# A first MLP product with high and low input halves side by side, and a gate moved from the weights to the output rows

## The chip, the cores and the metric

The kernel runs on one core of a Trainium2 chip. The metric is the device time of one execution in microseconds (us). A profile of one execution gives the span (first to last instruction) and every instruction's start and length on five engines: PE (TensorE, matrix products), DVE (VectorE), ACT (ScalarE), POOL (GpSimd) and SP (which issues most of the transfers). PEld stands for weight loads on TensorE.

## The reference, cut to what matters

```python
x = A_x                                             # 2048 x 512, float32
sa, ca, ga, sb, cb, gb = split(silu(c) @ w_mod, 6)  # six rows of 512
h = layernorm(x) * (1 + ca) + sa
x = x + ga * irfft2(rfft2(h) * (w_r + 1j * w_i))    # spectral filter
h = layernorm(x) * (1 + cb) + sb
act = mish(h @ w1 + b1)                             # w1: 512 x 1376; mish(u) = u * tanh(softplus(u))
x = x + gb * (act @ w2)                             # w2: 1376 x 512
```

The change is in the last two lines: the MLP and its gate `gb`.

## The kernel before, in words

The spectral part comes first: a forward transform, a product with the filter, and the back transform, whose last step (`p3_col`, `p3_row`) adds into x, which stays in SBUF as 16 row groups of 128 rows. While that last step runs (16 steps, from about 111 to 166 us), the kernel also prepares the MLP: `load_w1` and `split_w1`, `load_w2`, `gate_w2`, `split_w2` and `sum_w2` are spread over its steps by the table `prep`. Everything is in an order written out by hand: each engine runs its instructions in the order in which the code records them, and waits for semaphores where it needs another engine's result.

To multiply with nearly float32 accuracy at the rate of the format that TensorE reads faster (`F32R`), each operand is split into a high part (the value cast to that format) and a low part (the rest). Of the four products, high x high, low x high and high x low are kept.

The MLP works on 8 blocks of 256 rows. A block's hidden features (1376 = 10 x 128 + 96) are taken in 6 groups, t0 to t5, of which t0 has the tile of 96 and the others two tiles of 128. So there are 48 steps, and step s is done by `mlp(s)`. In it:

- `up(s)` (L720) is the first product: for each tile, 12 matmuls of 256 columns (three kinds of product, four parts of the 512 input features). Both tiles of a group fill the two halves of one PSUM bank with tag A, of which there are two.
- `mish(s)` (L730) reads that bank: ACT applies the activation with the bias to each tile (L736). For t1 to t5, DVE then makes four sums and differences of 128-wide pieces (L749): rows of a block and groups of features are combined so that `down` needs 7 products in place of 8. ACT casts the 7 pieces to their high parts (L755, two instructions), and `low` (L759, L761) takes the low parts on DVE.
- `down(s - 2)` is the second product for the group two steps back (L784; L770 for t0), which adds up over the block in six PSUM banks.
- In t1 the previous block is finished: `gather` (L787) copies four partial sums to `p` and `q` in SBUF on ACT, `residual` (L799, L802) adds the two others to x on DVE, and `spread` (L814) does the remaining additions into x on POOL: two between partial sums (L796, L797) and four into rows of x (L808 to L811). `store` sends both row groups out.
- In t3, `norm_pair` normalises the next block's two row groups on ACT (L141). In t4 and t5, `transpose_in` (L610) transposes half of them each, into an A bank and ahead of `up`, and `split_in` (L620) applies scale and shift on ACT (L625), takes the high part on DVE (L629) and the low part on DVE (L630).

The gate `gb` is a row of 512 factors, `gbr`, the same on every partition. It is multiplied into the rows of w2 as they are loaded: `gate_w2` (L677, L680) on POOL, 13 instructions of up to 128 x 512. What `down` makes is then already gated.

Small buffers come from a pool with two of each tag: `y` holds loaded rows of w2, `h` normalised rows and `p`, `q`, `g1` the activations, `g2` the sums. Whoever takes a third waits until the first is free. The end (`finish`, L847) does the last block's sums on DVE around the last `down`, whose products are taken without the 7-for-8 scheme (L777), with L691 giving the low parts of its weights.

## Time and profile before

| | us |
|---|---|
| median of 3 runs | 416.37 (414.9 to 416.45) |
| the profiled execution | 415.98 |
| its span | 414.2 |
| busy: PE, DVE, ACT, POOL | 394.8, 281.2, 220.8, 152.0 |
| mean granted TensorE clock | 0.989 |
| all transfers | 35.25 MB, a mean of 85 GB/s |

How to read what follows. The chain of work that ended last is followed back from the last instruction, at each step to what released it, and is shown in order of time: start, length, engine, output, line, number of instructions. A row of a timeline has start, length, engine, line, operation, output <- inputs, shapes and number of instructions; in brackets is the idle time of the engine ahead of it and what ended that. A row of a group of instructions ends with the busy time, the mean length of one in nanoseconds, and the idle time before them. A row of the page's slices has one digit for each fortieth of the span, the busy share in tenths. Rows with two times and a colon are stretches of time with the busy time of PE, PEld, DVE, ACT and POOL, the granted TensorE clock, and the transfers.

### The profile page before, as it was taken

The page shows a single profiled execution, that of the slowest core. Times are in us where ns is not written, and L with a number is a line of the kernel's source. Part 1 is how long each engine was busy: PE and PEld are TensorE (multiplying, and loading weights), DVE is VectorE, ACT ScalarE, POOL GpSimd, SP SyncE. Part 2 cuts the span into 40 slices and gives each one's busy share as a digit, 9 for nine tenths or more (in the row PEclk, how much of TensorE's full clock was granted, in tenths as well). Part 3 has the DMA queues.
Part 4 walks back from the last instruction along what each step waited for, and adds up shares of the span by engine and source line. Part 5 has one row for each costly group of instructions (what it writes and reads, how often), then busy time and mean ns, then how long its engine had stood idle before and what let it go on. Part 6 is the DMA issues. An engine that isn't in the chain of part 4 may idle for free.

```text
span 414.2 us, 8147 instructions
## 1 busy us (share of the span) xinstructions
PE 394.8 (95%) x3152; PEld 381.5 (92%) x3152; DVE 281.2 (68%) x542; ACT 220.8 (53%) x499; POOL 152.0 (37%) x180
## 2 busy tenths in 40 slices
PE   8999889999999899999999889999999999999996
PEld 8888778899899899899999789999999999999995
DVE  1999949686259999896854644673673772862854
ACT  1677754576746655655643653463472563553441
POOL 0677725576246975560500500410400500500520
PEclk9999999999999999999999969999999999999999
DMA  8999871371303322010100100010000000000021
GB/s 272 354 354 377 244 255 52 101 294 66 101 21 117 94 96 68 5 53 2 51 2 2 51 0 2 2 51 2 22 31 0 27 27 0 28 27 0 32 73 51
DMA packets 20902, 35.25 MB, mean 85 GB/s; under 512 B 3712, under 2 KB 6560, under 8 KB 20480
## 3 DMA queue, kind: packets, MB, share of 16 engines
q1 hardware_dynamic: 20432, 34.21, 24.3%
q8 instruction: 25, 0.41, 0.4%
q10 hardware_dynamic: 432, 0.53, 0.4%
q14 instruction: 13, 0.11, 0.1%
HBM read 30.53 MB, written 4.19 MB: 84 GB/s over the span
## 4 chain that ended last, share of the span: by engine, by line
PE 65%; DVE 23%; ACT 6%; issue 2%; DMA 2%; POOL 1%; SPq 0%; DVEq 0%; POOLq 0%; ACTq 0%
PE bank L727 26%; PE bank L784 21%; DVE st L112 4%; PE bank L456 3%; PE bank L502 3%; DVE ve L125 3%; DVE buf L749 2%; PE bank L770 2%; DVE x L651 2%; PE bank L489 2%; DMA x<-in_A_x_dram 2%; PE bank L435 1%; DVE w2a L691 1%; DVE buf L227 1%; DVE buf L207 1%
## 5 line engine op out<-in xcount | busy, mean ns | idle before, releaser
L761 DVE TENSOR_TENSOR al<-buf,ah 128x512 fp32r<-128x512 f32 (+2 forms) x87 | 64.6, 763 | 34.7 <-ACT ah L755 31.4
L755 ACT CAST ah<-buf 128x512 fp32r<-128x512 f32 (+2 forms) x87 | 46.1, 552 | 77.2 <-PE bank L784 34.8
L749 DVE TENSOR_TENSOR buf<-buf 128x128 f32<-128x128 f32 x156 | 56.8, 405 | 44.4 <-ACT buf L736 43.0
L796 POOL TENSOR_TENSOR buf<-buf 128x256 f32<-128x256 f32 x7 | 5.2, 738 | 163.4 <-ACT buf L791 163.4
L736 ACT ACTIVATE buf<-bank,b1n 128x256 f32<-128x256 f32 (+1 forms) x88 | 37.1, 468 | 41.8 <-PE bank L727 41.8
L727 PE MATMUL bank<-h,w1h 128*128 128x256 f32 (+1 forms) x352 | 55.0, 290 | 1.8 <-ACT buf L736 1.8
L727 PE MATMUL bank<-h2o,w1h 128*128 128x256 f32 (+1 forms) x352 | 53.5, 283 | 0.8 <-DVE h2o L629 0.8
L727 PEld LDWEIGHTS bank<-h,w1h 128*128 128x128 f32 (+1 forms) x352 | 47.9, 193 | 2.6 <-ACT buf L736 2.2
L727 PEld LDWEIGHTS bank<-h2o,w1h 128*128 128x128 f32 (+1 forms) x352 | 46.4, 186 | 1.3 <-DVE h2o L629 1.0
L784 PE MATMUL bank<-w2a,ah 128*128 128x256 f32 x168 | 36.3, 283 | 0.0
L784 PE MATMUL bank<-w2b,ah 128*128 128x256 f32 x161 | 34.4, 283 | 0.0
L727 PE MATMUL bank<-h,w1l 128*128 128x256 f32 (+1 forms) x176 | 28.8, 288 | 0.0
L784 PEld LDWEIGHTS bank<-w2a,ah 128*128 128x128 f32 x168 | 28.2, 191 | 0.0
L727 PE MATMUL bank<-h2o,w1l 128*128 128x256 f32 (+1 forms) x176 | 28.0, 282 | 0.0
L784 PEld LDWEIGHTS bank<-w2b,ah 128*128 128x128 f32 x161 | 26.8, 192 | 0.0
L680 POOL TENSOR_TENSOR buf<-buf,modr 128x512 f32<-128x512 f32 (+1 forms) x13 | 17.9, 1386 | 21.4 <-DMA buf<-in_B_w_dram 21.2
L234 PE MATMUL bank<-buf,mring 128*128 128x512 f32 x48 | 21.4, 445 | 4.2 <-DVE buf L227 1.9
L112 DVE BATCH_NORM_STATS2 st<-x 128x6 f32<-128x512 f32 x32 | 22.0, 688 | 5.0 <-DMA x<-in_A_x_dram 4.6
L638 PE MATMUL bank<-kc,d 128*128 128x128 f32 x128 | 24.8, 276 | 0.5 <-ACT d L360 0.5
L639 PE MATMUL bank<-kc,d 128*128 128x128 f32 x128 | 24.7, 275 | 0.0
L727 PEld LDWEIGHTS bank<-h,w1l 128*128 128x128 f32 (+1 forms) x176 | 24.6, 193 | 0.0
L727 PEld LDWEIGHTS bank<-h2o,w1l 128*128 128x128 f32 (+1 forms) x176 | 23.8, 186 | 0.0
(203 smaller groups left out, 1001.4 us busy)
## 6 DMA issues: line engine op xcount, KB each, us to landing
buf<-in_B_w_dram SPq DMA_DIRECT2D x20, 256.0 KB, 2.7
xring<-in_x_t_dram SPq DMA_DIRECT2D x16, 256.0 KB, 4.7
x<-in_A_x_dram SPq DMA_DIRECT2D x16, 256.0 KB, 5.0
wm<-in_w_mod_dram SPq DMA_DIRECT2D x16, 256.0 KB, 4.4
out_dram<-x SPq DMA_DIRECT2D x16, 256.0 KB, 2.0
mraw<-in_km_dram SPq DMA_DIRECT2D x16, 128.0 KB, 4.8
wqa<-in_w_q_dram SPq DMA_DIRECT2D x8, 256.0 KB, 4.2
wqb<-in_w_q_dram SPq DMA_DIRECT2D x8, 256.0 KB, 5.2
```

The source lines that it names most:

```text
L112: nc.vector.bn_stats(t, x[:, n, :])
L125: nc.vector.scalar_tensor_tensor(out, a, one, r, op0=op, op1=ALU.mult)
L234: nc.tensor.matmul(pa, m[:, a, 0:128], g, start=(i == 0), stop=False)
L638: nc.tensor.matmul(o, dj[:, 0:128], kc[0][:, n, :], start=True, stop=False)
L639: nc.tensor.matmul(o, dj[:, 64:192], kc[1][:, n, :], start=False, stop=True)
L680: nc.gpsimd.tensor_tensor(r, r, gbr[:r.shape[0]], op=ALU.mult)
L727: nc.tensor.matmul(ps[:rows, 256 * e:256 * e + 256], w[:, k, f * P:f * P + rows], h[:, k, :], start=(i == 0), stop=(i == 11))
L736: nc.scalar.activation(w[:rows, c], ps[:rows, c], AF.Mish, bias=b1n[:rows, f:f + 1])
L749: nc.vector.tensor_tensor(o, p, q, op=op)
L755: nc.scalar.copy(h, r)
L761: nc.vector.tensor_tensor(l, r, h, op=ALU.subtract)
L784: nc.tensor.matmul(o, a[p][:, e], w2[t][q][:, r], start=(half is None and t == 1 and i == 0), stop=(last and i == 2 and (n, half) != (1, 0)))
```

## The change

The first product takes its input with the high and low parts of each of the four feature parts side by side, as 512 columns. One matmul with the high weights makes high x high in the left half of a bank and high x low in the right half; a matmul of 256 columns with the low weights adds low x high to the left half. A tile takes 8 matmuls in place of 12 and fills a whole A bank. ACT then copies the right half with the bias to SBUF, DVE adds the left half, and one Mish on ACT works on both tiles in SBUF.

The gate no longer goes into w2: `gate_w2` is gone, and the rows that come out of the second product are multiplied by `gbr`. For that the output rows are put together apart from x: `own_rows` on DVE after `gather`, then in `chain` on POOL the other sums and two products with the gate, then `add_rows` adds to x on POOL. In the last block all of it is on DVE, and the last products are gated from PSUM.

The high part of the next block's input is taken on ACT in place of DVE. `transpose_in` stands behind `up` in place of ahead of it, and `split_in` between Mish and the casts. The steps of w2's preparation are moved: t1 by one step earlier, t2 and t3 by one or two, and the last split of t3 from after the loop to step 14.

```diff
     def h2_tiles(b):
         if b % 2 == 0:
-            h2[b] = [pm.tile([P, 4, 256], F32R, name=f"h2{i}", tag=f"h2{i}") for i in range(2)]
+            h2[b] = pm.tile([P, 4, 2, 256], F32R, name="h2e")
...
     def split_in(n, g):
-        hh, hl = (v[:, 2 * g:2 * g + 2, :] for v in h2[n // 2])
-        nc.vector.tensor_copy(hh, tv)
+        hh, hl = (h2[n // 2][:, 2 * g:2 * g + 2, i, :] for i in range(2))
+        nc.scalar.copy(hh, tv)
         nc.vector.tensor_tensor(hl, tv, plain(hh), op=ALU.subtract)
...
-    def gate_w2(t, *es):
-        for e in es:
-            r = st["w2", t][e]
-            nc.gpsimd.tensor_tensor(r, r, gbr[:r.shape[0]], op=ALU.mult)
...
     def up(g):
         b, t = divmod(g, NT)
-        ups[g] = ps = bank("C" if g < 2 else "A")
-        hh, hl = h2[b]
-        parts = [(w, h, k) for w, h in ((w1h, hh), (w1l, hh), (w1h, hl)) for k in range(4)]
+        h = h2[b]
+        ups[g] = []
         for e, f, rows in tiles(t):
-            for i, (w, h, k) in enumerate(parts):
-                nc.tensor.matmul(ps[:rows, 256 * e:256 * e + 256], w[:, k, f * P:f * P + rows], h[:, k, :],
-                                 start=(i == 0), stop=(i == 11))
+            ps = bank("C" if g < 2 and e == 0 else "A")[:rows]
+            fs = slice(f * P, f * P + rows)
+            for k in range(4):
+                nc.tensor.matmul(ps, w1h[:, k, fs], h[:, k], start=(k == 0), stop=False)
+            for k in range(4):
+                nc.tensor.matmul(ps[:, 0:256], w1l[:, k, fs], h[:, k, 0], start=False, stop=(k == 3))
+            ups[g].append((e, f, ps))

     def mish(g):
...
-        for e, f, rows in reversed(tiles(t)):
-            c = slice(256 * e, 256 * e + 256)
-            nc.scalar.activation(w[:rows, c], ps[:rows, c], AF.Mish, bias=b1n[:rows, f:f + 1])
+        for e, f, ps in ups.pop(g):
+            rows = ps.shape[0]
+            o = w[:rows, 256 * e:256 * e + 256]
+            nc.scalar.activation(o, ps[:, 256:], AF.Identity, bias=b1n[:rows, f:f + 1])
+            nc.vector.tensor_tensor(o, o, ps[:, 0:256], op=ALU.add)
+        o = w[:rows, 0:256 * e + 256]
+        nc.scalar.activation(o, o, AF.Mish)
...
-    def chain(b, eng):
-        p, q = done[b]
+    def own_rows(b):
+        r = buf("y"), buf("y")
+        nc.vector.tensor_tensor(r[1], out_ps[b][1], done[b][0], op=ALU.add)
+        nc.vector.tensor_copy(r[0], out_ps[b][2])
+        return r
+
+    def chain(b, eng, r):
+        p, q = done.pop(b)
         eng.tensor_tensor(q[:, 0:256], q[:, 0:256], p[:, 0:256], op=ALU.add)
         eng.tensor_tensor(q[:, 256:], q[:, 256:], q[:, 0:256], op=ALU.add)
...
+        both = q[:, 256:].unsqueeze(1).to_broadcast([P, 2, 256])
+        v = r[0].rearrange("p (j d) -> p j d", j=2)
+        if b == NB - 1:
+            eng.tensor_copy(v, both)
+        else:
+            eng.tensor_tensor(v, v, both, op=ALU.add)
+        eng.tensor_tensor(r[0][:, 256:], r[0][:, 256:], p[:, 256:], op=ALU.add)
...
+            eng.tensor_tensor(r[1][:, 256:], r[1][:, 256:], q[:, 0:256], op=ALU.add)
+            for t in r[::-1]:
+                eng.tensor_tensor(t, t, gbr, op=ALU.mult)
+
+    def add_rows(b, eng, r, rows=(1, 0)):
+        for i in rows:
+            n = 2 * b + i
+            eng.tensor_tensor(x[:, n, :], x[:, n, :], r[i], op=ALU.add)
...
     def mlp(s):
         b, t = divmod(s, NT)
         nxt = 2 * b + 2 if b < NB - 1 else None
+        up(s)
         if t in (4, 5) and nxt:
             transpose_in(nxt, t - 4)
-        up(s)
-        if t in (4, 5) and nxt:
-            split_in(nxt, t - 4)
         if t == 3 and nxt:
             norm_pair(nxt)
         parts = mish(s)
+        if t in (4, 5) and nxt:
+            split_in(nxt, t - 4)
+        parts = high(s, parts)
         down(s - LAG)
         if t == 1 and b:
             gather(b - 1)
-            residual(b - 1)
+            r = own_rows(b - 1)
         low(parts)
         if t == 1 and b:
-            spread(b - 1)
+            chain(b - 1, nc.gpsimd, r)
+            add_rows(b - 1, nc.gpsimd, r)
             store(b - 1)
...
     def finish():
...
-        own, ahead, far, both = rows_of(b)
-        chain(b, nc.vector)
-        far(nc.vector)
-        own(nc.vector)
-        both(nc.vector)
+        r = buf("y"), buf("y")
+        chain(b, nc.vector, r)
+        add_rows(b, nc.vector, r)
         down(total - 1)
-        residual(b, (0,))
-        store(b, (0,))
-        ahead(nc.vector)
-        residual(b, (1,))
-        store(b, (1,))
+        for i in range(2):
+            nc.vector.tensor_tensor(r[i], out_ps[b][2 - i], gbr, op=ALU.mult)
+            add_rows(b, nc.vector, r, (i,))
+            store(b, (i,))
...
-    for t, s in ((1, 1), (2, 6), (3, 11)):
-        for lag, fn, *args in ((-1, load_w2, t), (0, gate_w2, t, 0), (1, gate_w2, t, 1), (2, split_w2, t, False),
-                               (2, sum_w2, t, 0, 1), (3, sum_w2, t, 2, 3), (5, split_w2, t, True)):
-            if s + lag < N2:
-                prep[s + lag].append((fn, args))
...
+    for t, *at in ((1, 0, 2, 2, 3, 5), (2, 4, 8, 6, 7, 9), (3, 9, 11, 11, 12, 14)):
+        for s, fn, *args in zip(at, (load_w2, split_w2, sum_w2, sum_w2, split_w2), (t,) * 5,
+                                (None, False, 0, 2, True), (None, None, 1, 3, None)):
+            prep[s].append((fn, [a for a in args if a is not None]))
```

The new function `high` holds the casts that stood at the end of `mish`.

More of the change, by code (lines that the diff above doesn't have):

```diff
@@ L601, in h2_tiles @@
         if b % 2 == 0:
[L602 removed]
+            h2[b] = pm.tile([P, 4, 2, 256], F32R, name="h2e")
         else:
[L604 to L605 removed]
+            h2[b] = big.tile([P, 4, 2, 256], F32R, name="h2o", tag="cr")
     def norm_pair(n):
@@ L750, in mish, with high @@
             parts = [(w[:, P:], slice(0, 3)), (u, slice(3, 7))]
+        return parts
+    def high(g, parts):
+        hi, lo = acts[g] = [act.tile([P, 7, P], F32R, name=n) for n in ("ah", "al")]
         flat = []
@@ L792, in gather @@
         done[b] = p, q
-    def chain(b, eng):
-        p, q = done[b]
+    def own_rows(b):
[5 more added lines that the diff above has]
+        p, q = done.pop(b)
         eng.tensor_tensor(q[:, 0:256], q[:, 0:256], p[:, 0:256], op=ALU.add)
         eng.tensor_tensor(q[:, 256:], q[:, 256:], q[:, 0:256], op=ALU.add)
-    def residual(b, rows=(1, 0)):
-        for r in rows:
-            n = 2 * b + r
-            nc.vector.tensor_tensor(x[:, n, :], x[:, n, :], out_ps[b][2 - r], op=ALU.add)
@@ L900, in tile_spectral_block @@
             split_in(0, s - 7)
-    low(mish(0))
+    low(high(0, mish(0)))
     split_w2(0, False)
-    low(mish(1))
-    split_w2(3, True)
+    low(high(1, mish(1)))
     load_w2(4)
-    gate_w2(4, 0, 1)
     sum_w2(4, 0, 1, 2, 3)
@@ L922, in tile_spectral_block @@
             load_w2(5)
-            gate_w2(5, 0, 1)
         if s == total - 3:
```

36 lines of the change are left out of this document (10 added, 26 removed).

## The prediction, made before the changed kernel had run

> **What bounds the kernel now.** I read the page first, then the chain of work that ended last, then the timelines of one block of the MLP on each engine.
>
> ```profile
> PE 394.8 (95%) x3152; PEld 381.5 (92%) x3152; DVE 281.2 (68%) x542; ACT 220.8 (53%) x499; POOL 152.0 (37%) x180
> ...
> PE   8999889999999899999999889999999999999996
> ...
> PE 65%; DVE 23%; ACT 6%; issue 2%; DMA 2%; POOL 1%; SPq 0%; DVEq 0%; POOLq 0%; ACTq 0%
> ```
>
> The chain in order of time (start, length, engine, line, instructions):
>
> ```profile
> 296.08 1.38 PE bank L770 x6
> ...
> 323.70 2.84 PE bank L727 x24
> 326.54 1.38 PE bank L770 x6
> ...
> 330.76 2.52 PE bank L784 x21
> ...
> 407.45 2.76 PE bank L777 x12
> ```
>
> From about 186 us to the end the chain is almost only TensorE: `up` (L727) and `down` (L770, L784) back to back. A block of 256 rows takes 326.54 - 296.08 = 30.46 us. One 256-wide matmul takes 2.84/24 = 118 ns, a 512-wide one 1.38/6 = 230 ns, weight load included: the loads are hidden behind the streams.
>
> So the other engines matter only where TensorE waits for them. Their timelines around the first groups of the block's MLP (t1 to t3; t1 is the group in which the previous block is gathered):
>
> ```profile
> 321.02 0.28 PE L784 MATMUL bank<-w2c,ah 128*128 128x256 f32 x1
> 321.22 0.84 ACT L736 ACTIVATE buf<-bank,b1n 128x256 f32<-128x256 f32 x2 [2.50 <-PE bank L727]
> 322.09 1.02 DVE L749 TENSOR_TENSOR buf<-buf 128x128 f32<-128x128 f32 x4 [2.92 <-ACT buf L736]
> 323.66 1.04 ACT L755 CAST ah<-buf 128x384 fp32r<-128x384 f32 x2 [1.60 <-issue]
> 323.74 1.28 DVE L802 TENSOR_TENSOR x<-x,bank 128x512 f32<-128x512 f32 x2 [0.63 <-PE bank L784]
> 324.60 1.19 ACT L791 COPY buf<-bank 128x256 f32<-128x256 f32 x4
> 324.94 1.71 DVE L761 TENSOR_TENSOR al<-buf,ah 128x384 fp32r<-128x384 f32 x2
> 325.37 0.73 POOL L796 TENSOR_TENSOR buf<-buf 128x256 f32<-128x256 f32 x1 [24.25 <-ACT buf L791]
> 327.22 1.29 POOL L808 TENSOR_TENSOR x<-x,buf 128x512 f32<-128x512 f32 x1
> 328.58 0.75 POOL L809 TENSOR_TENSOR x<-x,buf 128x256 f32<-128x256 f32 x1
> 329.28 0.80 POOL L810 TENSOR_TENSOR x<-x,buf 128x256 f32<-128x256 f32 x1
> 330.16 1.43 POOL L811 TENSOR_TENSOR x<-x,buf 128x512 f32<-128x512 f32 x1
> 327.45 2.98 DVE L749 TENSOR_TENSOR buf<-buf 128x128 f32<-128x128 f32 x4 [0.80 <-ACT buf L736]
> 330.35 2.25 DVE L761 TENSOR_TENSOR al<-buf,ah 128x384 fp32r<-128x384 f32 x2
> 330.46 0.62 ACT L755 CAST ah<-buf 128x512 fp32r<-128x512 f32 x1 [2.16 <-DVE buf L749]
> 330.99 1.52 ACT L141 ACTIVATE buf<-x,nmr,rstd 128x512 f32<-128x512 f32 x2
> 339.59 1.21 DVE L761 TENSOR_TENSOR al<-buf,ah 128x384 fp32r<-128x384 f32 x2 [1.10 <-ACT ah L755]
> ```
>
> The reader is to see two things. First, while POOL works (325.37 to 331.59) the four 128-wide DVE operations of L749 take 2.98 us in place of 1.02, and the two of L761 take 2.25 in place of 1.21: a DVE operation with two SBUF inputs gets through about once per POOL instruction. Second, none of this reaches TensorE: the next `up` finds a free bank, since a group fills one A bank of two.
>
> An operation that reads PSUM is not held up in this way: 0.68 us, inside a POOL instruction of 2.25.
>
> ```profile
> 150.51 2.25 POOL L596 TENSOR_TENSOR w1l<-buf,w1h 128x512 fp32r<-128x512 f32 x1
> 151.56 0.68 DVE L651 TENSOR_TENSOR x<-x,bank 128x512 f32<-128x512 f32 x1
> ```
>
> The SBUF — State Buffer page of the Trainium skill (Who interferes with whom) says the same as a rule: a DVE instruction with two SBUF inputs and a GpSimd instruction that reads SBUF exclude each other for a whole instruction, while one with a PSUM input does not take part. The trace agrees (2.98 against 1.02, and 0.68). By that rule the sum below is +48 us; if a longer POOL stretch did not hold DVE at all, it would be the +9 of the second rival.
>
> **The change part by part.** Prices, by group of instructions:
>
> ```profile
> L736 ACT ACTIVATE buf<-bank,b1n 128x256 f32<-128x256 f32 x80 | 33.4, 468 | 39.1 <-PE bank L727 39.1
> L625 ACT ACTIVATE buf<-bank,cols 128x256 f32<-128x256 f32 x32 | 16.2, 556 | 0.0
> L802 DVE TENSOR_TENSOR x<-x,bank 128x512 f32<-128x512 f32 x16 | 10.4, 683 | 4.9 <-PE bank L784 4.4 <-PE bank L777 0.6
> L680 POOL TENSOR_TENSOR buf<-buf,modr 128x512 f32<-128x512 f32 x12 | 16.6, 1394 | 19.9 <-DMA buf<-in_B_w_dram 19.8
> ```
>
> *Matmuls.* 88 tiles of four pairs: 352 pairs of 256-wide matmuls become 352 of 512. A pair costs 2 x 118.3 - 230 = 6.6 ns less: -2.3 us, all on the path. An `up` of two tiles takes 2.78 us. The page TensorE: Matmul & The Clock Gate (Back-to-back issue gap) of the Trainium skill gives N/2.4 + 2.5 ns per matmul, by which a pair saves 2.5 ns and the whole 0.9 us; the trace has more, and the sum uses the trace.
>
> *New evacuation.* Each tile now has an Identity on ACT (256 from PSUM; L736: 0.47), an add on DVE (256, one PSUM input; under L802's 0.68 for 512, taken at 0.43), then one Mish for both tiles (512 in SBUF; between the 0.62 of the 512-wide cast and L736's pair of 0.84; taken at 0.68). ACT gains some 0.7 us a group, DVE 0.8, of a period of 5.3: throughput suffices. But a group now fills both A banks, so `up` of the next group needs the DVE add of this group's first tile. That add is queued on DVE behind the previous group's `low`, and its Identity on ACT behind the previous group's second cast, which waits for the four operations of L749.
>
> *The gate.* 13 gates of w2 leave POOL (13 x 1.39 = 18 us), and each of the 7 gathers gains two gates and two residual adds in place of the two 512-wide adds: 0.73 + 0.74 + 1.43 + 0.75 + 0.80 + 2 x 1.27 + 2 x 1.29 = 9.6 us instead of 6.2. On DVE, `own_rows` (0.68 + 0.65) stands where the two L802 stood, but needs the gathered rows, so it starts at 4.8 in place of 2.7 (323.74), ahead of `low`.
>
> Now the block, in us after the end of t1's `up` (321.02 = 0). ACT gathers until 4.8 as before (324.60 + 1.19). `own_rows` runs 4.8 to 6.1; `down` of t0 waits for it and ends at 6.9 in place of 6.7. The two `low` of t1 then alternate with POOL and end at 8.4; the add of t2's first tile ends at 8.8. **First stall:** `up` of t3 starts at 8.85, 1.9 late, and ends at 11.6; `down` of t1 ends at 14.15. t2's Mish ends at 10.0, when POOL is in its gates: the four L749 operations pass at the ends of the 1.3 us POOL instructions (in the rows above four passed over the three ends at 328.51, 329.33 and 330.08), at 11.0, 12.4, 12.65 and 14.2. Second cast until 14.9, the two norms of t3 (1.52) until 16.5, Identity 16.9, add 17.4. **Second stall:** `up` of t4 starts at 17.4 for 14.15: 3.25. If one operation passes per POOL instruction it is 18.5, if two, 16.0. **Third:** the transposes now stand behind `up` of t4 and want its first bank, whose add is still late: 1.2 (1.05 to 1.2). **Fourth:** in t5 the high part (0.62) is queued on ACT after Mish and two Identities (L625, 1.01), and the low part (about 0.68, as L802) behind it: ready 4.15 after the end of `up`, wanted by the next block's third 512-wide matmul at 0.44 + 2.52 + 0.46 = 3.42: 0.73. Before, it was ready with time to spare.
>
> Summed with the shorter matmuls, t1 to t1 takes 37.6 us in place of 30.5: **+7.1** (5.5 to 8.3). It is paid in blocks 1 and 3 to 6. Block 2 has a stall already, by the reload of activation tables:
>
> ```profile
> 222.99 0.28 PE L784 MATMUL bank<-w2c,ah 128*128 128x256 f32 x1
> ...
> 236.08 1.50 ACT L141 ACTIVATE buf<-x,nmr,rstd 128x512 f32<-128x512 f32 x2
> 236.94 0.33 PE L617 MATMUL bank<-ident,buf 128*128 128x128 f32 x1 [1.69 <-ACT buf L141]
> 239.79 1.22 PE L727 MATMUL bank<-h,w1h 128*128 128x256 f32 x4 [1.60 <-ACT buf L736]
> 239.79 5.38 PE bank L727 x24
> 240.00:242.00 2.00, 2.00 (x10) 2.00 (x11) 1.75 (x6) 1.45 (x4) 0.00 (x0) 0.50 0.00 0
> ```
>
> Its t1 ends at 222.99, so its norm starts 13.1 later and not 10.0 (330.99): 3.1 more, and `up` of t4 at 16.8. In the sum above that `up` would start at 17.4 + 3.1 = 20.5, less some 0.3 of waits that coincide, run at the same slow clock, and be followed by the transposes: 3.4 + 0.44 + 0.73 - 0.33, so +4.3. Block 7 has no norm and no transposes: the add of t3 waits for the two `low` of t2 alone and the second stall is 2.1; with the first (1.9), the later `down` (0.2), the split of the last w2 ahead of an add (0.3) and the shorter matmuls, +4.4.
>
> *End.* DVE now has ten operations where it had five, and a multiply ahead of each last add.
>
> ```profile
> 406.17 0.42 DVE L796 TENSOR_TENSOR buf<-buf 128x256 f32<-128x256 f32 x1
> ...
> 410.24 0.69 DVE L802 TENSOR_TENSOR x<-x,bank 128x512 f32<-128x512 f32 x1 [0.33 <-PE bank L777]
> ```
>
> From 406.17: six of 256 at 0.4, four of 512 at 0.65, then 4 x 0.65 = 7.6, so 413.7 in place of 410.93: **+2.8**.
>
> *Before the steady state.* In the transform stage (slices 11 to 16 of the page, some 55 us) 7 gates (9.7 us of POOL) and a cast of DVE go. TensorE is at 9 tenths or more in nearly all of these slices, so at most a tenth, 5 us, can be won: 0 to -5, taken at -2. In block 0 a split of w2 (1792 columns, so 3.5 casts of 0.62 and as many subtractions) stands on ACT and DVE ahead of the Identity and add for which the transposes now wait: about 2.2 each, partly hidden, +2 to +5, taken at +3 less the 0.3 of its matmuls.
>
> Loads of w2 move with their DMAs; the last one is issued behind the longer POOL chain, at about 15.3 + 0.4 of block 7, and lands before ACT is free at 20: no cost.
>
> Sum: 5 x 7.1 + 4.3 + 4.4 + 2.8 - 2 + 2.7 = +47.7, so the span 414.2 becomes about 462. The profiled execution took 415.98, 1.8 more than its span and 0.1% under the median 416.37: 463.7 by the same margin, given as **463 us**.
>
> **The rivals.** *The clock drops as well* (471 us, chance 0.15). In block 2 TensorE idled 1.69 + 1.60 within 5 us and then ran 24 matmuls in 5.38 us at a clock of 0.50. If the 3.25 us stall does the same in six blocks, each `up` after it costs 2.6 more, less the third stall that it swallows (1.2): 6 x 1.4 = +8. The page TensorE: Matmul & The Clock Gate of the Trainium skill (HAM oscillation) puts the limit at an idle window of about 3.4 us. The trace agrees for block 2, and no row shows a stall of 3.25 us. *The longer POOL chain does not hold DVE* (425 us). Then the first stall is 0.9, the second and third vanish, the fourth stays: 7 x (0.9 + 0.73 - 0.33) + 2.8 = 11.9, less the 2 to 3 us freed in the transform stage: +9. Against it stand the 2.98 and 2.25. *The bank wait is hidden* (414.5 us): if the first tile's add of t2 is done by 6.7 and that of t3 by 12, TensorE never waits, and what is left is -2.3 - 2.0 + 2.8 = -1.5. For it speaks the throughput (DVE and ACT have 2 us free a group); against it the order on DVE, where `own_rows` alone ends at 6.1 with two `low` (1.21) still ahead of the add.
>
> **How the numbers follow.** Forecast 0.63 (440 to 470, from 5 x 5.5 to 5 x 8.3 and the bounds of the small terms); clock 0.15; free DVE 0.14; hidden 0.08. The range must take in the first two and most of the third: 424 to 478. About 0.5% (2 us) is what a measurement of this kernel can tell, the runs of before spreading over 1.5. Hidden splits into 0.05 faster and 0.03 same; the rest, 0.92, is slower.
>
> **What would show it.** After: four pauses of TensorE a block, before the `up` of t3 (about 1.9, released by DVE's PSUM add), the `up` of t4 (3.2), the transposes (1.2) and in the next block's first `up` (0.7); 512-wide matmuls 230 ns apart; the POOL chain about 10 us long with L749's successor three times its free length. The prediction is wrong if the adds are not what TensorE waits for, or if the DVE operations pass POOL's gates freely.

## The result, and the profile after

The changed kernel takes 465.1 us (median; 464.28 to 465.94) against 415.63 us (414.84 to 416.45) for the kernel before, measured together: a ratio of 1.119, with a 95% interval from 1.1155 to 1.1226. It is slower by 49.5 us. The span of the profiled execution grew from 414.2 to 462.5 us.

From the page of the changed kernel: the busy times, two rows of the slices (TensorE's busy share and its granted clock, in tenths), and the shares of the chain that ended last.

```profile
PE 407.9 (88%) x2800; PEld 369.5 (80%) x2800; DVE 312.8 (68%) x620; ACT 259.5 (56%) x563; POOL 159.6 (35%) x188
...
PE   8999899999999997978985997998798799699694
...
PEclk9999999999999999997998899899899899999998
...
PE 44%; DVE 32%; ACT 16%; issue 4%; DMA 2%; POOL 1%; SPq 0%; DVEq 0%; ACTq 0%; POOLq 0%
```

TensorE has 352 matmuls less, yet it is busy for longer, at 8 tenths or less in half of the last 20 slices, and its clock is below 9 tenths in several of them. The chain that ended last now runs over DVE and ACT for 48% of the span.

What TensorE waited for (line <- what released it: us in total, times, longest), first before, then after:

```profile
PE bank L617 <- ACT buf L141: 2.3, 3, 1.7
...
PE bank L727 <- ACT buf L736: 1.8, 2, 1.6
```

```profile
PE bank L722 <- DVE buf L733: 31.8, 16, 5.7
PE bank L616 <- DVE buf L733: 2.7, 1, 2.7
PE bank L722 <- DVE h2o L629: 2.3, 4, 0.6
```

L733 is the new addition on DVE that frees the bank of a tile. `up` (now L722) waits for it 16 times and for 31.8 us. Before, the longest wait of TensorE in these steps was 1.7 us.

One block shows where the time sits. These are rows of the timelines of the changed kernel (start, length, engine, line; in brackets the idle time ahead and what ended it), with two stretches of time below them: busy time of PE, PEld, DVE, ACT and POOL, the granted clock, and the transfers.

```profile
352.34 0.74 POOL L802 TENSOR_TENSOR buf<-buf 128x256 f32<-128x256 f32 x1 [26.81 <-ACT buf L791]
356.26 0.74 DVE L733 TENSOR_TENSOR buf<-buf,bank 128x256 f32<-128x256 f32 x2
356.72 1.19 PE L722 MATMUL bank<-h2o,w1h 128*128 128x512 f32 x4 [1.43 <-DVE buf L733]
357.70 4.20 DVE L745 TENSOR_TENSOR buf<-buf 128x128 f32<-128x128 f32 x4 [0.70 <-ACT buf L735]
361.83 2.22 DVE L761 TENSOR_TENSOR al<-buf,ah 128x384 fp32r<-128x384 f32 x2
364.37 0.78 DVE L733 TENSOR_TENSOR buf<-buf,bank 128x256 f32<-128x256 f32 x2 [0.32 <-ACT buf L732]
364.84 1.20 PE L722 MATMUL bank<-h2o,w1h 128*128 128x512 f32 x4 [2.57 <-DVE buf L733]
369.17 0.74 PE L616 MATMUL bank<-ident,buf 128*128 128x128 f32 x4
379.21 0.70 PE L722 MATMUL bank<-h2e,w1h 128*96 128x512 f32 x2 [0.56 <-DVE h2e L629]
389.84 0.74 POOL L802 TENSOR_TENSOR buf<-buf 128x256 f32<-128x256 f32 x1 [26.81 <-ACT buf L791]
```

```profile
362.10:364.80 2.70, 0.17 (x2) 0.00 (x0) 2.38 (x4) 2.60 (x5) 0.93 (x1) 1.00 0.52 194
364.80:369.20 4.40, 4.36 (x17) 3.79 (x18) 2.83 (x8) 2.14 (x4) 0.00 (x0) 0.64 0.00 0
```

While POOL runs its chain, the four additions of L745 (the L749 of before) take 4.20 us in place of the 1.02 of a free engine, and the second additions of L733 come at 364.37. The `up` of t4 starts at 364.84, after 2.7 us in which TensorE did next to nothing, and then runs at a clock of 0.64: its 16 matmuls take until 369.17, 4.33 us. A block, from one first operation of POOL's chain to the next, takes 389.84 - 352.34 = 37.50 us.

The same first operation of the chain, in each of the blocks 1 to 7, cuts every run into comparable pieces. The table has the start of the first one and the distances between them (for the run without the chain, ACT's copy L791, which stands 0.8 us ahead of it). Blocks 3 to 6 agree within 0.1 us in all runs but the one with two more reads, whose 38.7 is the mean of 37.9 to 39.7.

| us | first | block 1 | block 2 | blocks 3 to 6, each | rest | span |
|---|---|---|---|---|---|---|
| before | 196.8 | 30.5 | 37.1 | 30.5 | 27.9 | 414.2 |
| after | 197.2 | 38.7 | 41.4 | 37.5 | 35.2 | 462.5 |
| product alone | 205.6 | 32.5 | 36.4 | 32.5 | 29.4 | 433.8 |
| gate alone | 190.9 | 32.1 | 39.3 | 32.2 | 31.4 | 422.5 |
| after, `low` first | 198.9 | 34.1 | 36.7 | 34.1 | 35.8 | 442.0 |
| after, two more reads | 196.8 | 37.7 | 42.8 | 38.7 | 39.4 | 471.6 |
| after, two fills | 198.5 | 37.4 | 41.0 | 37.5 | 36.8 | 463.7 |
| after, both orders | 196.8 | 34.1 | 36.6 | 34.1 | 35.9 | 439.8 |
| after, no POOL chain | 197.0 | 32.6 | 36.5 | 32.6 | 32.1 | 428.5 |
| gate, norms early | 192.4 | 31.2 | 38.0 | 31.2 | 31.3 | 417.7 |
| and scales early | 194.4 | 31.1 | 31.2 | 31.2 | 31.3 | 412.9 |
| and a short end | 193.9 | 31.2 | 31.2 | 31.2 | 30.5 | 411.6 |
| before, scales early | 201.6 | 30.5 | 30.5 | 30.5 | 27.9 | 412.3 |

The 48.3 us of the change are 0.4 ahead of the first chain, 8.2 in block 1, 4.3 in block 2, 4 x 7.0 in blocks 3 to 6, and 7.3 in block 7 and the end.

### The profile page after: what moved, and what is told of

Its sections match the earlier page's. It is cut to its first block, busy times and chain, and to the rows that moved or that the text cites. A ratio compares the mean times of both kernels' runs of the same rounds, so it can differ in the third digit from the quotient of the medians.

```text
span 462.5 us, 7587 instructions
## 1 busy us (share of the span) xinstructions
PE 407.9 (88%) x2800; PEld 369.5 (80%) x2800; DVE 312.8 (68%) x620; ACT 259.5 (56%) x563; POOL 159.6 (35%) x188
## 4 chain that ended last, share of the span: by engine, by line
PE 44%; DVE 32%; ACT 16%; issue 4%; DMA 2%; POOL 1%; SPq 0%; DVEq 0%; ACTq 0%; POOLq 0%
PE bank L784 12%; PE bank L722 12%; PE bank L724 6%; DVE buf L745 5%; DVE al L761 4%; DVE st L112 4%; ACT ah L755 3%; DVE buf L733 3%; PE bank L456 3%; PE bank L502 2%; DVE ve L125 2%; ACT buf L735 2%; ACT buf L141 2%; DVE x L650 2%; ACT buf L791 2%
## 5 line engine op out<-in xcount | busy, mean ns | idle before, releaser
L745 DVE TENSOR_TENSOR buf<-buf 128x128 f32<-128x128 f32 x156 | 62.5, 441 | 29.4 <-ACT buf L735 27.4
L755 ACT CAST ah<-buf 128x512 fp32r<-128x512 f32 (+2 forms) x87 | 46.0, 550 | 46.8 <-DVE buf L745 32.1
L722 PE MATMUL bank<-h2e,w1h 128*128 128x512 f32 (+1 forms) x176 | 53.3, 424 | 18.0 <-DVE buf L733 16.4
L722 PE MATMUL bank<-h2o,w1h 128*128 128x512 f32 (+1 forms) x176 | 53.3, 423 | 17.7 <-DVE buf L733 15.4
L733 DVE TENSOR_TENSOR buf<-buf,bank 128x256 f32<-128x256 f32 (+1 forms) x88 | 35.3, 416 | 38.6 <-ACT buf L732 38.4
L735 ACT ACTIVATE buf<-buf 128x512 f32<-128x512 f32 (+1 forms) x48 | 28.6, 597 | 44.7 <-DVE buf L733 44.6
L722 PEld LDWEIGHTS bank<-h2e,w1h 128*128 128x128 f32 (+1 forms) x176 | 31.6, 199 | 26.1 <-DVE buf L733 18.9
L722 PEld LDWEIGHTS bank<-h2o,w1h 128*128 128x128 f32 (+1 forms) x176 | 31.5, 199 | 26.1 <-DVE buf L733 18.0
L724 PEld LDWEIGHTS bank<-h2e,w1l 128*128 128x128 f32 (+1 forms) x176 | 29.0, 201 | 4.6
L724 PE MATMUL bank<-h2e,w1l 128*128 128x256 f32 (+1 forms) x176 | 30.0, 296 | 0.0
L637 PE MATMUL bank<-kc,d 128*128 128x128 f32 x128 | 24.8, 276 | 0.5 <-ACT d L360 0.5
```

Of the source, the lines that this page charges most:

```text
L637: nc.tensor.matmul(o, dj[:, 0:128], kc[0][:, n, :], start=True, stop=False)
L722: nc.tensor.matmul(ps, w1h[:, k, fs], h[:, k], start=(k == 0), stop=False)
L724: nc.tensor.matmul(ps[:, 0:256], w1l[:, k, fs], h[:, k, 0], start=False, stop=(k == 3))
L733: nc.vector.tensor_tensor(o, o, ps[:, 0:256], op=ALU.add)
L735: nc.scalar.activation(o, o, AF.Mish)
L745: nc.vector.tensor_tensor(o, p, q, op=op)
```

## The experiments

**The product alone.** The gate goes back into w2; what is left is the new first product, its evacuation, and the order of the steps around it.

```diff
+    def gate_w2(t, *es):
+        for e in es:
+            r = st["w2", t][e]
+            nc.gpsimd.tensor_tensor(r, r, gbr[:r.shape[0]], op=ALU.mult)
...
-            r = own_rows(b - 1)
+            residual(b - 1)
...
-            chain(b - 1, nc.gpsimd, r)
-            add_rows(b - 1, nc.gpsimd, r)
+            spread(b - 1)
```

> Only the first product is changed (side by side, Identity, add, Mish of both tiles, high input part on ACT, transposes behind up); the gate stays in w2 and POOL keeps its six operations of 6.2 us. Theory (two causes that need each other: a group that fills both A banks, and a POOL stretch of 10 us that holds DVE): POOL is done by 10.6 us after t1's up, so the add of t2's first tile is done by about 6.1 and up of t3 does not wait; up of t4 waits 0 to 1, the transposes about 1, the next block's first up 0.6: some +2 us a block, 428 us. Rival A (the filled banks alone cost it all): 455 us or more. Rival B (the longer POOL stretch alone costs it all): 416 us or less.

It took 435.53 us, a ratio of 1.0484 (1.0444 to 1.0524). A block takes 32.5 us, 2.0 more than before, and that part came as the theory had it. Another 8.8 us are lost ahead of the first chain, 205.6 against 196.8, which the theory had not. One of TensorE's waits in block 0, and what DVE did ahead of it (timelines):

```profile
169.78 1.21 DVE L690 TENSOR_TENSOR w2a<-modr,w2hi 128x1024 fp32r<-128x1024 f32 x1
170.91 0.74 DVE L738 TENSOR_TENSOR buf<-buf,bank 128x256 f32<-128x256 f32 x2
171.37 2.07 PE L727 MATMUL bank<-h2e,w1h 128*128 128x512 f32 x4 [2.41 <-DVE buf L738]
```

In block 0 the additions that free the banks (L738) stand on DVE behind the splits of w2 (L690). Ahead of the first chain TensorE waits 7.0 us for L738, and the four matmuls behind this wait take 2.07 us in place of about 0.92, at a clock of 0.50. So the product costs 20 us by itself, in a kernel whose POOL chain is the short one.

**The gate alone.** The kernel before, with the gate on the output rows.

```diff
-    def gate_w2(t, *es):
-        for e in es:
-            r = st["w2", t][e]
-            nc.gpsimd.tensor_tensor(r, r, gbr[:r.shape[0]], op=ALU.mult)
...
-            residual(b - 1)
+            r = own_rows(b - 1)
...
-            spread(b - 1)
+            chain(b - 1, nc.gpsimd, r)
+            add_rows(b - 1, nc.gpsimd, r)
```

> Only the gate is moved to the output rows, with the earlier preparation of w2; the first product, Mish from PSUM and the transposes are as before. Theory: DVE is held by POOL as long as in the changed kernel (four 128-wide operations in about 4.2 us), but a group fills one A bank of two, so TensorE does not see it: 0.25 us a block for down of t0, 2.9 us at the end, and 3 to 4 us won in the transform stage: 416 us, between 413 and 419. Rival A: the same, 416. Rival B (the POOL stretch alone): 440 us or more.

It took 424.15 us, a ratio of 1.0201 (1.0173 to 1.0229): over the range expected. The transform stage does give time back, more than expected (190.9 in place of 196.8: 5.9 us), but each block loses 1.7. TensorE's main wait, and the rows of one block:

```profile
PE bank L617 <- ACT buf L141: 5.5, 7, 3.2
```

```profile
330.66 3.07 DVE L744 TENSOR_TENSOR buf<-buf 128x128 f32<-128x128 f32 x4
333.76 0.62 ACT L750 CAST ah<-buf 128x512 fp32r<-128x512 f32 x1 [3.69 <-DVE buf L744]
334.28 1.52 ACT L141 ACTIVATE buf<-x,nmr,rstd 128x512 f32<-128x512 f32 x2
335.85 0.55 PE L617 MATMUL bank<-ident,buf 128*128 128x128 f32 x3 [0.38 <-ACT buf L141]
```

The longer chain on POOL does reach TensorE without the new product, by a path that the expectation had overlooked: the held additions (L744) make ACT's second cast late, the two norms (L141) are queued behind that cast, and the transposes, which here stand ahead of `up`, wait for the norms.

The two parts alone cost 19.9 and 8.5 us, 28.4 together. The whole change costs 49.5. The other 21 us come from their meeting: by the table the blocks 1 to 6 lose 41 us with both parts and 20 with the parts added up.

**`low` ahead of the own rows.** The whole change; in t1, DVE takes the two low parts first and the own rows after them.

```diff
         if t == 1 and b:
             gather(b - 1)
-            r = own_rows(b - 1)
         low(parts)
         if t == 1 and b:
+            r = own_rows(b - 1)
             chain(b - 1, nc.gpsimd, r)
```

> The changed kernel with the low parts of t1 recorded ahead of own_rows on DVE in place of behind it. Theory (order on DVE makes the first pause, POOL's stretch the second): the low parts are done by about 5 us after t1's up, the add of t2's first tile by 6.6, so the pause before up of t3 goes from 1.8 to 0; the one before up of t4 goes from 2.6 to about 2, short enough that the clock stays up after it; some 3 us a block less, 445 us. If the order on DVE does not matter: 465.

It took 443.1 us (1.0656; 1.0607 to 1.0706), 22 less than the changed kernel, and a block takes 34.1 us. That order alone is worth 3.4 us a block, the slow clock that no longer comes included. The wait of t3's `up` is gone (0.4 is left ahead of `down` of t0), that of t4's `up` is 0.7, the transposes behind it wait for 1.7, and the clock stays at 1.00 through the block.

```profile
346.81 1.20 PE L722 MATMUL bank<-h2o,w1h 128*128 128x512 f32 x4 [0.52 <-DVE buf L733]
351.46 0.66 PE L616 MATMUL bank<-ident,buf 128*128 128x128 f32 x4 [1.58 <-DVE buf L733]
```

```profile
337.94:372.07 34.13, 31.24 (x209) 28.00 (x208) 21.91 (x47) 19.52 (x41) 10.19 (x9) 1.00 0.04 16
```

**Two more POOL instructions, reading or only writing.** Two runs lengthen POOL's chain by two instructions in each block, whose output nothing uses: two products of the gate row with itself, or two fills with zero of the same 128x512.

```diff
+            for _ in range(2):
+                nc.gpsimd.tensor_tensor(spare, gbr, gbr, op=ALU.mult)
```

> The changed kernel with two more 512-wide POOL products per block, of the gate with itself into a tile that nobody reads, behind the last addition of rows into x. No other instruction needs their result. Theory (DVE's operations with two SBUF inputs are held while POOL reads SBUF): the low parts of t2 pass later, the pause before up of t4 grows by 1.3 to 2.7 us a block, 475 to 485 us. Rival (DVE waits for results of the POOL chain or its buffers): no change, 465 us.

```diff
+            for _ in range(2):
+                nc.gpsimd.memset(spare, 0.0)
```

> The changed kernel with two more POOL instructions in each block's chain, like the run with two more reads, but these two only write: they fill a tile of 128x512 that nothing reads. Nothing of the computation is changed. Theory (VectorE's operations with two inputs in SBUF are held by those POOL instructions that read SBUF): filling needs no read, so VectorE is held as in the changed kernel; span 462 to 465, time 464 to 468, and the time under 'bank L.. <- DVE' stays near the 31.8 us of the changed kernel. Rival (any POOL instruction, or a longer POOL queue by itself, holds them, because the norms and row additions come late): as with two more reads, 472 to 476, and near 40 us under that wait.

With two more reads: 474.85 us (1.142; 1.1356 to 1.1483), just under the range expected. With two fills: 465.43 us (1.1192; 1.1161 to 1.1223), the time of the changed kernel. DVE's held rows, the added instructions and the main wait of TensorE, first with the reads, then with the fills:

```profile
359.17 5.33 DVE L746 TENSOR_TENSOR buf<-buf 128x128 f32<-128x128 f32 x4 [0.70 <-ACT buf L736]
364.41 2.83 DVE L762 TENSOR_TENSOR al<-buf,ah 128x384 fp32r<-128x384 f32 x2
364.31 2.39 POOL L856 TENSOR_TENSOR spare<-modr 128x512 f32<-128x512 f32 x2
```

```profile
PE bank L723 <- DVE buf L734: 40.1, 16, 6.8
```

```profile
361.43 2.23 DVE L762 TENSOR_TENSOR al<-buf,ah 128x384 fp32r<-128x384 f32 x2
362.58 1.10 POOL L856 MEMSET spare<- 128x512 f32 x2
```

```profile
PE bank L723 <- DVE buf L734: 31.9, 16, 5.7
```

DVE's low parts take 2.23 us with the fills beside the second of them, as they took 2.22 without. Beside the added reads they take 2.83 us, and 3.07 in two of the seven blocks. A fill does not hold them; the reads do. The SBUF — State Buffer page of the Trainium skill (Who interferes with whom) says that a DVE instruction with two SBUF inputs contends with a GpSimd instruction that reads SBUF and not with one that only writes it; these two runs agree. They don't match fully in length (1.10 against 2.39 us), so a hold of up to 1.1 us by the fills would have been the other outcome, and it isn't seen.

Not all of the 9.7 us that the reads cost is such a hold. In five of the seven blocks the four additions take 5.33 us in place of 4.20, and nearly all of that is over before the first added product starts (364.31). The first addition and POOL's first gate start within 0.01 us of each other in every block of both kernels; in these five the addition takes 1.43 us, elsewhere 0.29. What decides that is not shown. The hold that can be put down to the added reads themselves is the 0.6 to 0.85 us of the low parts.

**The whole change without POOL's chain.** This is the measure of all that POOL does to the changed kernel. It leaves out the sums, the gate and the additions into x for seven blocks, so its output lacks them.

```diff
-            chain(b - 1, nc.gpsimd, r)
-            add_rows(b - 1, nc.gpsimd, r)
+            done.pop(b - 1)
             store(b - 1)
```

> The changed kernel without POOL's chains in blocks 1 to 7: the sums of the gathered parts, the gate on the rows and the addition to the rows of x are left out, and those rows are stored without the MLP's part. VectorE still makes the own rows in the same place and order, ACT its copies. Theory (what costs the 7 us a block is POOL holding VectorE): the direct 2.3 us stay won, and of the stalls only what the order on VectorE makes by itself remains: t1's two low parts end at 4.9 + 1.3 + 1.4 = 7.6 after t1's product instead of 8.4, the first addition near 8.0 instead of 8.8, a stall of about 1 us; the second, 2.6 us, goes and with it the slow clock behind it, the one at the next block's start (0.6) stays: a period of 28.2 + 1.0 + 0.6 = 29.8 us. With seven blocks and the last one's gate chain: 412 (407 to 420). Rival (the added work and order on VectorE and ACT make the stalls without POOL): a period of 34 or more, 440 or more.

It took 431.21 us (1.0361; 1.032 to 1.0401), between the two numbers. The expectation has a slip: it takes the 2.3 us of shorter matmuls, which the prediction has for the whole kernel, as a gain in each block. With 0.3 us a block the theory's own stalls give 30.2 + 1.0 + 0.6 = 31.8 us a block, and the run has 32.6. The waits of TensorE in it, and rows of one block:

```profile
PE bank L722 <- DVE buf L733: 6.4, 10, 2.5
PE bank L616 <- DVE buf L733: 6.0, 7, 2.7
```

```profile
335.24 1.20 PE L722 MATMUL bank<-h2o,w1h 128*128 128x512 f32 x4 [0.33 <-DVE buf L733]
336.21 1.02 DVE L745 TENSOR_TENSOR buf<-buf 128x128 f32<-128x128 f32 x4 [0.70 <-ACT buf L735]
```

So the theory was 0.8 us a block short, and the rival's 34 or more is not reached. The four additions are back at 1.02 us, and the clock is 1.00 all through the block. So of the 7.0 us that a block loses, POOL's chain accounts for 37.5 - 32.6 = 4.9, the slow clock included. The other 2.1 are there without any POOL work: the order on DVE and ACT makes `up`, the transposes and the next block's first `up` wait by some 2.4 us, for a gain of 0.3 or less in the matmuls. Over the kernel POOL's chain is worth 34.0 of the 48.3 us (spans 462.5 and 428.5).

**The norms early.** Two runs move the norms from the block's fourth step to its first, out from behind the cast that waits for POOL; `gather` uses other buffers (`t`) so that `h` is free.

```diff
-        p, q = buf("h"), buf("h")
+        p, q = buf("t"), buf("t")
...
-        if t == 3 and nxt:
-            norm_pair(nxt)
...
         low(parts)
+        if (t == 0 or s == LAG) and nxt:
+            norm_pair(nxt)
```

> The gate alone (old first product, gate on the output rows), with one thing moved: the two norms on ACT that feed the next block's transposes are issued at the end of the block's first step instead of its fourth (in block 0 in its first step that runs in the loop), and the gathered sums use the t buffers so that h is free for them. Theory (the 1.7 us that the gate alone loses in each block reaches TensorE through the norms: POOL holds VectorE, so ACT's second cast waits for a buffer, the norms stand behind it and the transposes behind them): the period falls from 32.18 us back to 30.5, seven blocks give back 11 to 12 us of the 422.5, the 5.9 us won in the transform stage now stay: 412 (410 to 415), under the kernel before. Rival (VectorE held by POOL holds TensorE through the Mish output buffers all the same): period 31.5 or more, 418 or more.

With the gate alone it took 419.17 us (1.0072; 1.0048 to 1.0096). A block falls to 31.2 us, between the two expectations, while the time lies in the rival's range; the waits for the norms are gone. The sum missed 412 for two reasons, by the table: 1.5 us are lost ahead of the first chain, and a block gives back 1.0 of the 1.7 us. Against the kernel before stands, too, the longer end, 31.3 in place of 27.9.

For the remaining 0.7 us the timelines show two places, of some 0.4 each. `down` of t0 starts late, behind the own rows; and ACT's second cast still waits for held additions, with the scaling of the transposed rows (L625) and t4's Mish (L731) queued behind it, which frees the bank that t5's `up` wants.

```profile
336.30 0.62 ACT L750 CAST ah<-buf 128x512 fp32r<-128x512 f32 x1 [3.40 <-DVE buf L744]
337.74 0.83 ACT L731 ACTIVATE buf<-bank,b1n 128x256 f32<-128x256 f32 x2
338.62 0.74 PE L722 MATMUL bank<-h2o,w1h 128*128 128x256 f32 x4
```

> The whole change, with both orders that the runs point to: t1's low parts ahead of the own rows on VectorE (as in the run that reached 443), and the norms in the block's first step instead of the fourth. Theory: the own rows ahead cost 3.4 us a block and were taken out there; what is left of 34.13 - 30.5 = 3.6 us a block is the low parts held by POOL, which reach TensorE partly through the norms (waits of the transposes on ACT's order), partly through the additions that free the banks. The norms give back about 1 us a block: 436 (432 to 440). Rival (the additions alone hold it): 442 to 444.

With the whole change and `low` first it took 442.36 us (1.0637; 1.06 to 1.0674). A block takes 34.1 us, as without the move: the rival holds. With the new product the norms are not what holds TensorE in this order; the additions that free the banks are.

**The scales early.** Block 2 is longer than its neighbours in both kernels, since the last four rows' scales (Ln and Exp) make ACT change its table there (three loads of 1.28 us in the kernel before, at 233.07, 234.68 and 237.60). Two runs move them ahead of the first Mish.

```diff
+    norm_scale(N2 - 4, N2)
     low(mish(0))
...
-        if s == 2 * NT + 2:
-            norm_scale(N2 - 4, N2)
```

> The run before it (gate alone, norms in the first step) with the last four rows' scales (the Ln and Exp on ACT, which cost block 2 a longer period than its neighbours: 37.1 us against 30.5 in the kernel before) computed once ahead of the first MLP block's first Mish. Theory: block 2's extra 6.6 us go, of which 2 to 3 come back ahead of the first block, where ACT now changes its function table: 408 (405 to 411). Rival (the change of table costs the same wherever it stands, because the first Mish waits for it too): no gain, 412.

On top of the gate and the early norms it took 414.8 us (0.9971; 0.9954 to 0.9987): 4.4 less than the run before, as the theory had the gain, from a higher start. Block 2 falls from 38.0 to 31.2, and 2.0 come back ahead of the first chain.

> The kernel before with one thing moved: the last four rows' scales (Ln and Exp on ACT, in block 2) computed once ahead of the first MLP block's first Mish, as in the gate's run that reached 414.8. Theory (that run's gain over the one before it, 4.4 us, came from this move alone and has nothing to do with the gate): block 2's 6.6 us go, 2.0 come back ahead of the first block: 411.3 (409.5 to 413). Rival (it pays only where block 0 has slack from the gate's earlier w2 preparation): 414 to 417.

On the kernel before, with nothing of the change, it took 412.76 us (0.9921; 0.9893 to 0.9949). Block 2 falls to 30.5; ahead of the first chain 4.8 us come back and not 2.0. There the table is now loaded right before the first Mish:

```profile
164.51 1.28 ACT L736 ACT_TABLE_LOAD   x1
```

**A short end.** The gate's best run, with the last block's gate applied to the finished rows.

```diff
+        nc.scalar.copy(r[1][:, 0:256], out_ps[b][0][:, 0:256])
         chain(b, nc.vector, r)
-        add_rows(b, nc.vector, r)
         down(total - 1)
         for i in range(2):
-            nc.vector.tensor_tensor(r[i], out_ps[b][2 - i], gbr, op=ALU.mult)
+            nc.vector.tensor_tensor(r[i], r[i], out_ps[b][2 - i], op=ALU.add)
+            nc.vector.tensor_tensor(r[i], r[i], gbr, op=ALU.mult)
             add_rows(b, nc.vector, r, (i,))
```

> The gate's run with norms and scales early, and another end for the last block: there the gate is applied once to the finished rows (sum, product, addition to x: three operations a row after the last product), and not to the chain's parts and to the last products each (two gate operations more on each row in two of three pieces); one copy of a quarter row goes to ACT. VectorE's work from the gathered parts to the last store was 401.97 to 409.64, 7.7 us, for 2.8 us of TensorE; by the durations of its rows the new list is 5 operations of the chain (2.2) and six of 0.6 (3.7), 5.9 us. Theory: 1.6 us less, 413.2 (412 to 414.5). Rival (the last two rows' own operations after the last product set the end either way, and are now three instead of two): 414.8 to 416.

It took 413.76 us (0.9947; 0.9917 to 0.9976). The rest behind the last chain is 0.8 shorter, half of what was expected: the six operations start at 404.12, 0.2 after their product, and follow each other every 0.7 us, not 0.6.

```profile
404.12 0.69 DVE L856 TENSOR_TENSOR buf<-buf,bank 128x512 f32<-128x512 f32 x1 [0.19 <-PE bank L772]
```

So with three things around it moved, the gate on the rows is no slower than the kernel before. But one of these moves, the scales, has nothing to do with the gate, and on the kernel before it is as good or better by itself (0.9921 against 0.9947, intervals overlapping): no run shows a gain from the gate. No run that has the new first product and does the whole computation came below 433.8 us of span.

## Why the prediction was right

The forecast of 463 us rests on four pauses of TensorE in each block, and the profile after shows three of them where it put them, with the releasers that it named. Their sizes, and the slow clock that it had as a rival, come out as follows (one block, in us after the end of t1's `up`, which is 348.04 here).

| step of the prediction | predicted | measured |
|---|---|---|
| `up` of t3, first stall with the wait ahead of it | starts 8.85, 1.9 + 0.2 | 8.7, 2.0 |
| the four additions (L749, now L745) done | 14.2 | 13.9 |
| `up` of t4, second stall | starts 17.4, 3.25 | 16.8, 2.7 |
| third stall, at the transposes | 1.2 | 0 |
| slow clock behind the second stall | 0 | 1.5 in `up`, and 0.2 after it |
| fourth stall, the next block's first `up` | 0.73 | 0.7 |
| matmuls | -0.3 | -0.2 |
| a block (3 to 6) | +7.1 | +7.0 |
| block 1 | +7.1 | +8.2 |
| block 2 | +4.3 | +4.3 |
| block 7 and the end | 4.4 + 2.8 | 7.3 |
| ahead of the first chain | -2 + 2.7 | +0.4 |

The forecast's own terms for a block add up to 7.0 and not 7.1 (1.9 + 0.2 + 3.25 + 1.2 + 0.73 - 0.3), half a microsecond over the kernel.

*What held.* POOL's chain takes 10.7 us (352.34 to 363.03; predicted about 10), and its gates hold the four additions, about one per POOL instruction: four in 4.20 us, as in the forecast's sum (10.0 to 14.2). The two-bank argument held: TensorE waits for L733 in every block, and without POOL's chain it still does (6.4 and 6.0 us in the run without the chain). The fourth stall and the end were right to 0.1 us: the last product now starts at 452.67 and the last addition ends 6.5 us later, against 3.6 before (407.29 to 410.93).

```profile
452.67 0.63 PE L777 MATMUL bank<-w,ah 128*128 128x512 f32 x2
...
458.51 0.69 DVE L824 TENSOR_TENSOR x<-x,buf 128x512 f32<-128x512 f32 x1
```

*What was off inside the block, and cancelled.* The second stall was 0.55 too long: the additions came 0.3 earlier, and the cast and the norms behind them followed each other more closely than their lengths. The third stall doesn't exist as a wait: the forecast let `up` of t4 run at full clock and the transposes then wait for its bank. In fact `up` runs for 4.33 us at the slow clock, and by its end the bank is free. So the first rival was half right. The clock does drop behind the second stall, in blocks 1 and 3 to 6. In blocks 3 to 6 it costs 1.7 us where the rival had 2.6, and swallows the third stall as the rival said, so a block costs 0.5 and not 1.4 more than the forecast's pauses, and the shorter second stall takes that back. A forecast of "pauses at full clock" was not how it went; that the sum came out the same is luck. The remark under this rival that the trace agrees for block 2 does not hold either: TensorE had waited 1.69 and 0.38 us there, with 0.33 us of work between, when the clock fell, and the wait of 1.60 us came after.

*Ahead of the first block* two terms were mis-sized with opposite signs. By the end of the second `up` the changed kernel is 3.2 us ahead (159.4 against 162.7; predicted 2, at most 5; the gate alone won 5.9 to the first chain), and block 0 lost 3.6 (predicted 2.7), with 4.1 us of waits for L733. That these two nearly cancel is luck too.

*Block 1* costs 1.2 more than its neighbours, by the clock alone: behind the same pause it loses 3.0 us there in place of 1.7 (below). In the run with two fills block 1 takes 37.4 us like its neighbours.

*The second rival*, that the longer chain on POOL doesn't hold DVE, falls with the low parts beside the added reads (2.83 to 3.07 us, against 2.23 beside fills) and with the run without the chain (34 us less). But the prediction's own account of the gate was too narrow: it put POOL's effect on the path only through the new additions. The gate alone shows a second path, through cast, norms and transposes, of 1.7 us a block. *The third rival*, that the bank wait is hidden, falls with the product alone (4.8% slower).

## What to carry to other kernels

Where an engine with slack in its mean evacuates a bank, ask what stands ahead of the evacuation in that engine's queue at the moment the bank is wanted: here the addition that frees a bank takes 0.4 us, and TensorE waited 31.8 us for it because other operations, most of them held by POOL, stood before it in the queue (6.4 us are left without POOL's chain). Price a move of work to POOL by the DVE operations with two SBUF inputs that will run beside it, and follow what is queued behind them on the other engines, not only the operations themselves. And parts of a change that meet in one stretch don't add: 20 and 8.5 us apart were 49.5 together, partly because a pause that is short with either part became long enough to slow the clock.

## What the runs showed of the hardware

*A pause of 2.1 us can drop the clock, one of 2.5 us need not, and what a drop costs varies.* In the changed kernel the pause ahead of t4's `up` is 2.7 us in block 1 and in blocks 3 to 6; without the end of the last matmul it is 2.5 to 2.6 us of idle time, the figure in brackets in the rows. Stretches behind it, first in block 1, then in the block shown above (the number after POOL's is the granted clock):

```profile
209.60:211.00 1.40, 1.37 (x3) 1.17 (x4) 0.67 (x3) 1.00 (x2) 0.00 (x0) 0.50 0.00 0
...
215.00:215.60 0.60, 0.60 (x5) 0.60 (x4) 0.00 (x0) 0.44 (x1) 0.00 (x0) 0.50 0.00 0
```

```profile
364.80:365.80 1.00, 0.96 (x4) 0.82 (x5) 0.35 (x1) 0.61 (x1) 0.00 (x0) 1.00 0.00 0
365.80:367.50 1.70, 1.70 (x9) 1.46 (x8) 1.46 (x5) 1.12 (x4) 0.00 (x0) 0.57 0.00 0
367.50:369.20 1.70, 1.70 (x8) 1.51 (x7) 1.02 (x2) 0.40 (x2) 0.00 (x0) 0.50 0.00 0
```

In block 1 the clock is at a half from the moment work resumes and stays there for about 6 us, so `up` and the transposes are slow throughout; in the other it falls 1 us after work has resumed and stays low for about 3.5 us.

Other runs show that the length of the pause does not decide it alone. Behind idle times of 2.05 us (`low` first, block 7), 2.10 (both orders, block 7) and 2.14 (two fills, block 7) the clock fell to a half; behind 2.13 in block 7 of the changed kernel and 2.47 in block 2 of the run without the chain it stayed at 1.00. First a stretch behind the pause with both orders, then the pause without the chain and a stretch behind it:

```profile
420.45:422.00 1.55, 1.54 (x4) 1.26 (x5) 0.82 (x4) 1.14 (x2) 0.00 (x0) 0.50 0.04 11
```

```profile
239.16:241.63 2.47, 0.00 (x1) 0.01 (x1) 1.13 (x6) 2.45 (x6) 0.00 (x0) 1.00 0.00 0
242.60:244.70 2.10, 2.10 (x13) 1.67 (x12) 1.21 (x5) 1.51 (x4) 0.00 (x0) 1.00 0.00 0
```

Single pauses of 1.6 us and less left it at 1.00 in these runs (1.4 in the changed kernel, 1.6 with `low` first). In block 2 of the kernel before, 1.69 and 0.38 us of waiting with 0.33 us of work between them were enough for a drop to 0.50. The page TensorE: Matmul & The Clock Gate of the Trainium skill (HAM oscillation) puts the limit at gaps of more than about 3.4 us. These runs don't agree with that limit: 2.7 us were enough in five blocks, and 2.1 us in three others. The same page (What's actually happening) has the window run freely, independent of the kernel, which would fit a drop that comes at once in one block, late in others and not at all in a third; no run here tested that.

*A fill on POOL did not hold DVE*, as said above (2.23 us beside it, 2.22 without), while beside two products of the same shape DVE's low parts take 2.83 to 3.07.

*A 512-wide matmul saves less than it seemed.* An `up` of two tiles went from 2.84 to 2.81 us, so the direct gain of the new product is about 1.3 us over the kernel (40 such steps of 0.03, and 8 with one tile), where 2.3 was predicted. The second tile's four 512-wide matmuls are 237 ns apart in this block (346.62 to 347.57), the first tile's 230.

```profile
345.23 1.09 PE L722 MATMUL bank<-h2o,w1h 128*128 128x512 f32 x4
...
347.57 0.63 PE L724 MATMUL bank<-h2o,w1l 128*128 128x256 f32 x4
```

The last of these four end at 347.57 + 4 x 0.118 = 348.04.
